# A chunked linear-attention kernel with two gated layers: the queries' table of powers moves to PSUM and scales seven chunks of keys backwards on DVE

## The chip, the cores and the metric

The kernel runs on one core of a Trainium2 chip. The metric is the device time of one execution in microseconds (us). The core's engines each run their own instructions in order: TensorE (PE, with PEld loading weights), VectorE (DVE), ScalarE (ACT), GpSimd (POOL), and SyncE (SP), which issues all transfers here.

## The reference, cut to what matters

```python
# attention with per-channel decay: B=4, 8 heads, S=768, 48 channels per head
for t in range(S):
    cur = einsum('bhd,bhe->bhde', u * k_t, v_t)
    y[:, :, t] = einsum('bhd,bhde->bhe', r_t, state + cur)
    state = w * state + einsum('bhd,bhe->bhde', k_t, v_t)
x = y laid out as (B, S, 384)
# first layer: u, v = halves of relu(x @ w_in); v is normalised over its channels
v_s = einsum('ts,bsd->btd', w_spatial, v_n) + b_spatial
x = (u * v_s) @ w_out
# second layer: h = relu(x @ w_in2); convolution of 3 taps along the sequence
out = (h * sigmoid(conv(h))) @ w_out2
```

Everything is fp32. Each large product of the layers is computed from split operands (a rounded part and its remainder), as three matmuls into one accumulation.

## The kernel before, in words

The attention goes through 24 chunks of 128 positions, six for each of four batches. Chunk n has two tiles: `ld` (queries and keys with channels on partitions, 112 x 2 x 4 x 128) and `nat` (queries, keys and values with positions on partitions). Three of each are in flight; the load of chunk n+3 is issued after chunk n's last matmul.

The decay inside a chunk is put into the operands. `tables` (L508) fills TT in SBUF: TT[:, 0] holds w^(t-64) for the queries, TT[:, 1] w^(63-s) for the keys. `scaled` (L569) multiplies the queries of chunk n by TT[:, 0] on DVE (L574); `scaled_k` (L581) multiplies the keys by TT[:, 1] on POOL (L583), but for chunk 0, where DVE does both at once (L578). Then:

- `products` (L211, line L216) writes keys times queries into two PSUM banks, `pa0` and `pa1`, one for each head of a pair;
- `masked` (L618, line L621) copies what lies on the allowed side of the diagonal from `pa` to `aT` on DVE; `aT` was filled by ACT (L254) with the diagonal that belongs to `u`;
- `outer` (L235, line L239) writes keys times values of the chunk into the bank `pu`; `state` (L677) adds it to `zc` on DVE (L683, L685), ACT writes it to `zbd` (L245), and POOL applies the decay (L692);
- `from_state` (L219, line L222) and `from_chunk` (L225, line L231) build the output in the bank `py`; ACT and DVE split it into `ys` and `xT` (L658 to L662), and a part of it goes through DRAM: a write to `yd` (L667), then two reads into `xT` (L672).

The first layer has `s1` (L720, half of w_in, one chunk at a time, then a normalisation on DVE and ACT), `s2` (L764, the other half), `s3` (L784, the spatial product) and `s4` (L810); the second layer has `s5` (L887) and `s6` (L933). The weights come as 64-bit words in disguise: DVE converts a block of them in four instructions (L427 to L430, tile `wy`), and ACT and POOL split it (L362, L364).

The program is written out by a planner (class `Order`): every piece of work is a generator that names the engine and a cost, waits for keys (`need`) and free slots (`take`), and the planner emits instructions in the order in which its model starts them. So a change in what waits for what changes the order of all five engines. Until a planned time of 62 us the planner fills gaps on PE with matmuls whose result is not used (`keep_warm`, L558, line L565). All eight PSUM banks are in use: three for the layers (`ps_m`), one for the weight conversion, `pa0`, `pa1`, `py` and `pu`.

Of the kernel before, what the change touches and what calls it, by code (L numbers as in the profile page):

```python
# [26 lines left out]
class Order:  # L27
# [58 lines left out]
    def spawn(self, g, rank=1, at=None):  # L86
        self._go(g, rank, self.t if at is None else at, None)
# [61 lines left out]
class Net:  # L149
# [26 lines left out]
            fill=0.0, base=0, channel_multiplier=-1)  # L176
        nc.gpsimd.memset(self.zbd, 0.0)

    def att_psum(self, ps):
        C, NP = self.C, self.NP  # L180
        self.pa = [ps.tile([C, NP, C], F32, name=f"pa{i}") for i in range(2)]
        self.py = ps.tile([self.R, NP, C], F32, name="py")
        self.pu = ps.tile([self.R, NP, self.D], F32, name="pu")
        self.nc.vector.memset(self.py, 0.0)
        self.nc.vector.memset(self.pu, 0.0)

    def powers(self, asc, dsc, n):

# [159 lines left out]
    def run(self, xd=None):  # L348
# [130 lines left out]
        if xd is None:  # L479
            ac = right("ac", 1)  # L480
            ld_p, nat_p = right("ld", 3), right("nat", 3)
            ew_p, at_p, ys_p = right("ew", 2), right("at", 2), right("ys", 2)
            TT = ac.tile([R, 2, NP, C], F32, name="TT")
            W128 = ac.tile([R, NP, 1], F32, name="W128")
            mask = ac.tile([C, C], U32, name="mask")
            maskb = mask.rearrange("c (o t) -> c o t", o=1).to_broadcast([C, NP, C])
            yd = dram.tile([n_chunks, R, 2 * C], F32, name="yd")
            W128b = W128.to_broadcast([R, NP, D])
# [19 lines left out]
        def tables():  # L508

            asc = x2_p.tile([R, NP, HALF + 1], F32, tag="x2", name="asc")  # L510
            dsc = x2_p.tile([R, NP, HALF + 1], F32, tag="x2", name="dsc")
            wt = ew_p.tile([R, 4, NP], F32, tag="wt", name="wt")
            dw = t_p.tile([R, NP, R], F32, tag="t", name="dw")
            wr, w2, m, wk = (wt[:, i] for i in range(4))
            m = m.bitcast(U32)
            iv = ew_p.tile([R, NP, 1], F32, tag="iv", name="iv")
            nc.sync.dma_start(out=wr, in_=self.wq)
            nc.gpsimd.memset(dsc[:, :, HALF:HALF + 1], 1.0)
            self.att_consts(ac)
            nc.sync.dma_start(out=self.uB, in_=self.u.broadcast_to([C, DM]))  # L520
            nc.vector.memset(asc[:, :, 0:1], 1.0)

            nc.vector.memset(wk, 1.0)
            self.att_psum(att.enter_context(tc.tile_pool(name="ps_a", bufs=1, space=PSUM)))

            for _ in range(4):
                nc.tensor.matmul(
                    out=self.pa[1][0:R, :, 0:R], lhsT=self.zbd[:, 0], rhs=self.zbd, start=True, stop=True)
            nc.vector.tensor_tensor(w2, wr, wr, ALU.mult)
            nc.vector.tensor_scalar(m, w2, W2_MIN, None, ALU.is_ge)  # L530
            nc.vector.scalar_tensor_tensor(m, w2, W2_MAX, m, ALU.is_le, ALU.mult)
# [7 lines left out]
            nc.vector.tensor_tensor(TT[:, 0, :, 0:HALF], asc[:, :, 0:HALF], ivb, ALU.mult)
            nc.vector.tensor_tensor(TT[:, 1, :, HALF:C], dsc[:, :, 1:HALF + 1], ivb, ALU.mult)  # L540
            nc.scalar.activation(out=TT[:, 0, :, HALF:C], in_=asc[:, :, 0:HALF], func=ACTF.Copy)
            nc.scalar.activation(out=TT[:, 1, :, 0:HALF], in_=dsc[:, :, 1:HALF + 1], func=ACTF.Copy)

            for p in range(NP):
                nc.scalar.activation(
                    out=dw[:, p], in_=self.ident[0:R, 0:R], func=ACTF.Copy, scale=W128[:, p])
            self.transpose_table(TT[:, 1], dw)

        def masks():
            yield gps(3 * C, 3)  # L550
# [17 lines left out]

        def scaled(n):  # L569
            yield need(("ldd", n))  # L570
            if n:
                spawn(scaled_k(n), rank(n))
                yield dve(NP * C)
                nc.vector.tensor_tensor(ld[n][:, 0], ld[n][:, 0], TT[:, 0], ALU.mult)  # L574
                done(("lq", n))
            else:
                yield dve(2 * NP * C)
                nc.vector.tensor_tensor(ld[n], ld[n], TT, ALU.mult)  # L578
                done(("lq", n), ("lk", n))

        def scaled_k(n):  # L581
            yield gps(NP * C)
            nc.gpsimd.tensor_tensor(ld[n][:, 1], ld[n][:, 1], TT[:, 1], ALU.mult)  # L583
            done(("lk", n))

        def bonus(n):
# [21 lines left out]

        def att_a(n):
            yield need(("lq", n), ("lk", n))  # L610
            yield need(("A", n - 1, 0), ("A", n - 1, 1))
            yield od.pairs(1.0)
            self.products(ld[n][:, 0], ld[n][:, 1])
            for x in range(2):
                spawn(masked(n, x), rank(n))
            yield FORK

        def masked(n, x):  # L618
# [5 lines left out]
        def att_v(n):  # L624
            b, c = divmod(n, NCH)
            on = c < NCH - 1
            yield need(("lq", n), ("kn", n), ("z", n - 1))
            if on:
                yield od.pairs(0.45)
                self.outer(nat[n][:, 1], nat[n][:, 2])  # L630
                spawn(state(n), rank(n))
            yield need(("y", n - 1))
            if c:
                yield od.pairs(1.0)
                self.from_state(ld[n][:, 0])
            done(("mix", n))
            yield need(("A", n, 0), ("A", n, 1))
            if c % HC == 0:
                yield take(x_f)
            yield take(ys_f)  # L640
# [36 lines left out]
        def state(n):  # L677
            first = n % NCH == 0
            if not first:
                yield need(("zw", n - 1))  # L680
            yield dve(NP * D)
            if first:
                nc.vector.tensor_copy(out=self.zc, in_=self.pu)  # L683
            else:
                nc.vector.tensor_tensor(self.zc, self.zc, self.pu, ALU.add)  # L685
            yield need(("mix", n))
            yield act(2 * NP * D, 2)
            self.set_state()
            done(("z", n))
            if n % NCH < NCH - 2:  # L690
                yield gps(NP * D)
                nc.gpsimd.tensor_tensor(self.zc, self.zc, W128b, ALU.mult)  # L692
                done(("zw", n))
# [263 lines left out]
                        break  # L957
                spawn(g, rank(i))

        done(("A", -1, 0), ("A", -1, 1), ("z", -1), ("y", -1))  # L960
# [40 lines left out]
        if xd is None:  # L1001
# [121 lines left out]
```

## Time and profile before

| what | value |
|---|---|
| three runs | 602.73, 599.0, 602.54 us (median 602.54) |
| profiled execution | 605.17 us, of which the span of instructions 603.1 us |
| PE busy | 577.6 us (96%), 3980 matmuls |
| DVE / ACT / POOL busy | 382.3 (63%) / 356.5 (59%) / 291.2 us (48%) |
| mean granted TensorE clock | 0.976 |

The times of the runs are of separate executions; the profiled one is 2.6 us longer than their median. In the tables of the trace, "idle before" is the time in which an engine stood still just before an instruction, with what released it. The granted clock of TensorE is a share of full speed: 1.00 is 2.4 GHz, 0.50 is 1.2 GHz, and values between are means over a stretch.

### The profile page before, as it was taken

How to read it: one execution, taken by the hardware profiler on the slowest of the kernel's cores; microseconds unless marked ns; L12 is line 12 of the kernel's file. 1: busy time of each engine (PE TensorE's matmuls, PEld its weight loads, DVE VectorE, ACT ScalarE, POOL GpSimd, SP SyncE). 2: the span in 40 equal slices, each digit the busy share in tenths (PEclk: the TensorE clock that was granted, in tenths of full speed). 3: DMA queues.
4: the chain of work that ended last, by engine and by line, in shares of the span. 5: the costliest groups of instructions: out<-in, count | busy, mean ns of one | idle time of the engine just before them, and what ended most of it. 6: DMA issues, size and time to landing. Idle time of an engine off the chain costs nothing.

```text
span 603.1 us, 11155 instructions
## 1 busy us (share of the span) xinstructions
PE 577.6 (96%) x3980; PEld 546.3 (91%) x3980; DVE 382.3 (63%) x864; ACT 356.5 (59%) x877; POOL 291.2 (48%) x315
## 2 busy tenths in 40 slices
PE   6999969999999999999999999999999999999992
PEld 3999858999888999888999999999999999999991
DVE  4889878867679847778665533675546455564701
ACT  3558766736586456486354524487667666675810
POOL 5688877855858329468414240254223243232410
PEclk8999969999999999999999999999999999999997
DMA  8676545546565456285346714340221303120010
GB/s 219 209 218 210 153 158 163 172 140 212 156 194 195 114 165 217 57 265 160 120 166 238 261 59 139 150 158 27 93 84 49 106 13 106 57 76 27 15 39 33
DMA packets 49316, 81.29 MB, mean 135 GB/s; under 512 B 5601, under 2 KB 40930, under 8 KB 48866
## 3 DMA queue, kind: packets, MB, share of 16 engines
q1 hardware_dynamic: 49250, 80.48, 42.3%
q8 instruction: 33, 0.54, 0.4%
q14 instruction: 33, 0.27, 0.1%
HBM read 57.27 MB, written 23.20 MB: 133 GB/s over the span
## 4 chain that ended last, share of the span: by engine, by line
PE 88%; POOL 3%; DMA 3%; DVE 2%; issue 1%; ACT 1%; SPq 0%; ACTq 0%; DVEq 0%; POOLq 0%
PE s L887 17%; PE s L933 17%; PE s L784 15%; PE s L720 9%; PE s L810 8%; PE s L764 7%; PE pa L216 4%; PE warm L565 4%; PE py L231 4%; PE py L222 2%; DMA ld<-in_rkT_dram 1%; PE pu L239 1%; DMA nat<-in_rkv_dram 1%; POOL nat L591 1%; POOL ld L583 1%
## 5 line engine op out<-in xcount | busy, mean ns | idle before, releaser
L364 POOL TENSOR_TENSOR g<-g,g 128x384 fp32r<-128x384 f32 x64 | 64.6, 1014 | 122.6 <-ACT g L362 122.6
L887 PE MATMUL s<-xl,wi 128*128 128x386 f32 x576 | 108.1, 340 | 0.0
L933 PE MATMUL s<-wo,g 128*128 128x384 f32 x576 | 107.0, 339 | 0.0
L784 PE MATMUL s<-wsp,vn 128*128 128x384 f32 x576 | 104.3, 337 | 0.4 <-POOL vn L364 0.4
L887 PEld LDWEIGHTS s<-xl,wi 128*128 128x128 f32 x576 | 102.5, 189 | 0.0
L933 PEld LDWEIGHTS s<-wo,g 128*128 128x128 f32 x576 | 102.1, 188 | 0.0
L784 PEld LDWEIGHTS s<-wsp,vn 128*128 128x128 f32 x576 | 99.7, 188 | 2.4 <-POOL vn L364 0.8
L900 DVE SCALAR_TENSOR_TENSOR c<-h,cw,c 128x384 f32<-128x384 f32 x64 | 39.7, 621 | 57.6 <-ACT c L898 57.6
L254 ACT ACTIVATE aT<-ident,dg 128x128 f32<-128x128 f32 x192 | 60.1, 392 | 9.3 <-DVE dg L249 9.0
L364 POOL TENSOR_TENSOR gat<-u,gat 128x384 fp32r<-128x384 f32 x32 | 32.6, 1027 | 53.7 <-ACT gat L362 49.4
L720 PE MATMUL s<-wi,xT 128*128 128x512 f32 x216 | 57.2, 415 | 0.0
L764 PE MATMUL s<-xT,wi 128*128 128x384 f32 x288 | 54.7, 338 | 0.0
L810 PE MATMUL s<-gat,wo 128*128 128x384 f32 x288 | 53.3, 337 | 0.0
L764 PEld LDWEIGHTS s<-xT,wi 128*128 128x128 f32 x288 | 50.0, 188 | 1.0 <-ACT zbd L245 0.2
L810 PEld LDWEIGHTS s<-gat,wo 128*128 128x128 f32 x288 | 50.0, 188 | 0.6 <-ACT zbd L245 0.2
L720 PEld LDWEIGHTS s<-wi,xT 128*128 128x128 f32 x216 | 41.6, 198 | 9.5 <-issue 0.2
L903 ACT ACTIVATE c<-c 128x384 f32<-128x384 f32 x64 | 29.7, 465 | 31.5 <-DVE c L901 31.5
L907 DVE TENSOR_TENSOR g<-h,c 128x384 f32<-128x384 f32 x64 | 35.2, 551 | 19.9 <-ACT c L903 18.8
L895 ACT ACTIVATE h<-s 128x386 f32<-128x386 f32 x64 | 31.3, 489 | 17.1 <-PE s L887 15.9
L901 DVE SCALAR_TENSOR_TENSOR c<-h,cw,c 128x384 f32<-128x384 f32 x64 | 39.9, 623 | 2.3
L591 POOL TENSOR_TENSOR nat<-nat 128x384 f32<-128x384 f32 x24 | 24.9, 1039 | 31.6 <-DMA nat<-in_rkv_dram 23.3
L364 POOL TENSOR_TENSOR stg<-stg 128x192 fp32r<-128x192 f32 (+1 forms) x34 | 19.8, 587 | 41.2 <-ACT stg L362 35.7
(103 smaller groups left out, 932.1 us busy)
## 6 DMA issues: line engine op xcount, KB each, us to landing
nat<-in_rkv_dram SPq DMA_DIRECT2D x24, 576.0 KB, 4.2
ld<-in_rkT_dram SPq DMA_DIRECT2D x24, 448.0 KB, 5.4
xl<-x2d SPq DMA_DIRECT2D x8, 1155.0 KB, 6.1
x2d<-x SPq DMA_DIRECT2D x24, 384.0 KB, 3.0
stg<-in_w_out_dram SPq DMA_DIRECT2D x24, 192.0 KB, 2.8
out_dram<-o SPq DMA_DIRECT2D x24, 192.0 KB, 1.9
stg<-in_w_in_dram SPq DMA_DIRECT2D x12, 256.0 KB, 3.9
wo2d<-stg SPq DMA_DIRECT2D x16, 192.0 KB, 1.9
```

The costliest lines, as they stand in the source:

```text
L254: self.nc.scalar.activation(out=a[:, x, h // 2], in_=self.ident, func=ACTF.Copy, scale=d[:, h:h + 1])
L364: nc.gpsimd.tensor_tensor(dst[1], src, dst[0].bitcast(F32), ALU.subtract)
L720: nc.tensor.matmul(out=ps, lhsT=xt[:, k, l], rhs=wi[:, k, r, UF:DFF], start=(k == 0 and (l, r) == PARTS[0]), stop=(k == KD - 1 and (l, r) ...
L764: nc.tensor.matmul(out=ps, lhsT=wi[:, k, l, f * 128:(f + 1) * 128], rhs=xT[b, h][:, k, :, r], start=(k == 0 and (l, r) == PARTS[0]), stop= ...
L784: nc.tensor.matmul(out=ps, lhsT=vn[:, s, l, f * 128:(f + 1) * 128], rhs=wsp[:, s, r, h * HT:(h + 1) * HT], start=(s == 0 and (l, r) == PAR ...
L810: nc.tensor.matmul(out=ps, lhsT=wo[:, k, l, m * 128:(m + 1) * 128], rhs=gat[b, h, k][:, r], start=(k == 0 and (l, r) == PARTS[0]), stop=(k ...
L887: nc.tensor.matmul(out=ps, lhsT=late["wi2"][:, k, l, f * 128:(f + 1) * 128], rhs=xl[j][:, k, r], start=(k == 0 and (l, r) == PARTS[0]), st ...
L895: nc.scalar.activation(out=h, in_=ps, func=ACTF.Relu)
L900: nc.vector.scalar_tensor_tensor(c, h[:, 0:HT], cw[:, f, 0:1], c, ALU.mult, ALU.add)
L901: nc.vector.scalar_tensor_tensor(c, h[:, 2:HT + 2], cw[:, f, 2:3], c, ALU.mult, ALU.add)
L907: nc.vector.tensor_tensor(g, h[:, 1:HT + 1], c, ALU.mult)
L933: nc.tensor.matmul(out=ps, lhsT=g2[j][:, k, l, t * 128:(t + 1) * 128], rhs=late["wo2"][:, k, r], start=(k == 0 and (l, r) == PARTS[0]), st ...
```

## The change: what it does

1. The queries' table moves to a PSUM bank, `TQ`; the keys' table stays in SBUF as `TK`.
2. Read backwards, TQ gives w^(63-s), the keys' powers. For chunks 0 to 6 DVE scales queries and keys in two instructions, both with TQ; from chunk 7 on POOL scales the keys with TK, as before.
3. TQ takes the bank of `pu`. The outer product now goes into the first 192 columns of `pa0`. So `outer` of chunk n has to wait until `masked` has copied `pa0` of chunk n (key `("A", n, 0)`), and `products` of chunk n+1 until `zc` has taken the outer product (new key `("zc", n)`).
4. `outer` becomes a piece of its own (`att_o`), in one chain with `att_a` (the products).

```diff
-    def att_psum(self, ps):
+    def att_psum(self, ps, own=True):
         self.pa = [ps.tile([C, NP, C], F32, name=f"pa{i}") for i in range(2)]
         self.py = ps.tile([self.R, NP, C], F32, name="py")
-        self.pu = ps.tile([self.R, NP, self.D], F32, name="pu")
...
+        else:
+            pu = self.pa[0].rearrange("c p t -> c (p t)")[0:self.R, 0:NP * self.D]
+            self.pu = pu.rearrange("r (p d) -> r p d", p=NP)
...
-            TT = ac.tile([R, 2, NP, C], F32, name="TT")
+            TK = ac.tile([R, NP, C], F32, name="TK")
...
+            TQ = TT["q"] = ps_a.tile([R, NP, C], F32, name="TQ")
...
         def scaled(n):
             yield need(("ldd", n))
-            if n:
+            late_k = n >= 7
+            if late_k:
                 spawn(scaled_k(n), rank(n))
+            yield dve(NP * C)
+            nc.vector.tensor_tensor(ld[n][:, 0], ld[n][:, 0], TT["q"], ALU.mult)
+            done(("lq", n))
+            if not late_k:
                 yield dve(NP * C)
-                nc.vector.tensor_tensor(ld[n][:, 0], ld[n][:, 0], TT[:, 0], ALU.mult)
-                done(("lq", n))
-            else:
-                yield dve(2 * NP * C)
-                nc.vector.tensor_tensor(ld[n], ld[n], TT, ALU.mult)
-                done(("lq", n), ("lk", n))
+                nc.vector.tensor_tensor(ld[n][:, 1], ld[n][:, 1], TT["q"][:, :, ::-1], ALU.mult)
+                done(("lk", n))
...
         def att_a(n):
             yield need(("lq", n), ("lk", n))
-            yield need(("A", n - 1, 0), ("A", n - 1, 1))
+            yield need(("A", n - 1, 0), ("A", n - 1, 1), ("zc", n - 1))
...
+        def att_o(n):
+            if n % NCH == NCH - 1:
+                done(("zc", n), ("o", n))
+                return
+            yield need(("kn", n), ("A", n, 0))
+            yield od.pairs(0.45)
+            self.outer(nat[n][:, 1], nat[n][:, 2])
+            done(("o", n))
+            spawn(state(n), rank(n))
+            yield FORK
...
         def att_v(n):
             yield need(("lq", n), ("kn", n), ("z", n - 1))
-            if on:
-                yield od.pairs(0.45)
-                self.outer(nat[n][:, 1], nat[n][:, 2])
-                spawn(state(n), rank(n))
...
-            yield need(("A", n, 0), ("A", n, 1))
+            yield need(("A", n, 0), ("A", n, 1), ("o", n))
...
+            done(("zc", n))
...
-            for g in (att_a, att_v):
-                spawn(od.chain([(g(n), rank(n)) for n in range(n_chunks)]), 0)
+            for gs in ((att_a, att_o), (att_v,)):
+                spawn(od.chain([(g(n), rank(n)) for n in range(n_chunks) for g in gs]), 0)
```

The planner's new order differs on every engine. Three places matter. In the rows, the matmuls of `products` alternate between `pa_159` (pa0) and `pa_160` (pa1), four of each for a chunk; a line of "..." leaves out the repeats.

PE at the end of the first batch, before: from the last matmuls of chunk 5 (`py`) to the second of the two `s1` products (tiles s_1066 and s_1171) that end batch 0.

```order
L231 MATMUL py<-aT,nat 48x128 x8
L216 MATMUL pa_159<-ld 128x128
...
L239 MATMUL pu<-nat 48x48 x8
L720 MATMUL s_1066<-wi,xT 128x512 x9
L231 MATMUL py<-aT,nat 48x128 x8
L216 MATMUL pa_159<-ld 128x128
...
L239 MATMUL pu<-nat 48x48 x8
L720 MATMUL s_1171<-wi,xT 128x512 x9
```

The same place in the changed kernel (the two `s1` products are s_1069 and s_1155):

```order
L227 MATMUL py<-ld,zbd 112x128 x4
L574 MATMUL warm<-ident 128x128 x2
L236 MATMUL py<-aT,nat 48x128 x8
L738 MATMUL s_1069<-wi,xT 128x512 x9
L221 MATMUL pa_159<-ld 128x128
...
L738 MATMUL s_1155<-wi,xT 128x512 x9
L244 MATMUL pa_159<-nat 48x48 x8
```

The second `s1`, which works on chunk 5's own output, now comes after one `s1` and one set of products; before, two sets of products, one `py`, two outer products and one `s1` stood between. Over the whole order the matmuls of L565 rise from 98 to 112.

DVE in the same stretch, before: the two masked copies of chunk 5 follow each other, and between those of chunk 6 stand the statistics of `s1` and a scaling of queries.

```order
L621 COPY_PREDICATED aT<-mask,pa_159 128x512
L621 COPY_PREDICATED aT<-mask,pa_160 128x512
...
L621 COPY_PREDICATED aT<-mask,pa_159 128x512
L733 BN_STATS s_1105<-v 128x6
L734 BN_AGGR mv<-s_1105 128x2
L736 TENSOR_SCALAR rs<-mv 128x1
L574 TENSOR_TENSOR ld<-ld,TT 112x512
L621 COPY_PREDICATED aT<-mask,pa_160 128x512
```

DVE in the changed kernel: the masked copies of chunk 5, then the scalings of chunk 6's queries (L584) and keys (L588).

```order
L642 COPY_PREDICATED aT<-mask,pa_159 128x512
L432 TENSOR_SCALAR wy<-stg 128x192
...
L435 SCALAR_TENSOR_TENSOR stg<-stg,wy 128x192
L642 COPY_PREDICATED aT<-mask,pa_160 128x512
...
L584 TENSOR_TENSOR ld<-ld,TQ 112x512
L254 TENSOR_REDUCE dg<-nat 128x8
L678 TENSOR_TENSOR ys<-py,ys 112x128
L679 TENSOR_TENSOR xT<-py,xT 112x3x128
L588 TENSOR_TENSOR ld<-ld,TQ 112x512
```

A block of four weight conversions now stands between the copies of chunk 5, and the statistics no longer stand between those of chunk 6.

PE in the third batch, before, around chunk 13's output (first row) and the state product of chunk 14 (L222):

```order
L231 MATMUL py<-aT,nat 48x128 x8
L764 MATMUL s_2232<-xT,wi 128x384 x9
L239 MATMUL pu<-nat 48x48 x8
L222 MATMUL py<-ld,zbd 112x128 x4
L231 MATMUL py<-aT,nat 48x128 x8
```

And in the changed kernel:

```order
L236 MATMUL py<-aT,nat 48x128 x8
L244 MATMUL pa_159<-nat 48x48 x8
L227 MATMUL py<-ld,zbd 112x128 x4
L221 MATMUL pa_159<-ld 128x128
```

The `s2` product that stood between chunk 13's output and the outer product of chunk 14 has moved away.

## Rows read from the trace of the kernel before

**Rows 1.** The page, part 1: busy us (share of span) x instructions.

```profile
PE 577.6 (96%) x3980; PEld 546.3 (91%) x3980; DVE 382.3 (63%) x864; ACT 356.5 (59%) x877; POOL 291.2 (48%) x315
```

**Rows 2.** Waits of PE: who waited for whom, total us, times, longest.

```profile
PE py L231 <- DVE rs L740: 5.0, 1, 5.0
...
PE pa L216 <- POOL vn L364: 1.5, 1, 1.5
PE pa L216 <- POOL gat L364: 1.2, 1, 1.2
```

**Rows 3.** Stretches: us, busy time by engine, granted clock (PEclk), DMA.

```profile
12.40:14.60 2.20, 2.09 (x17) 1.90 (x17) 0.50 (x2) 1.74 (x6) 2.14 (x4) 0.50 1.03 298
18.00:20.00 2.00, 2.00 (x19) 1.98 (x18) 1.86 (x5) 0.85 (x3) 1.62 (x3) 0.98 0.33 118
73.00:74.40 1.40, 0.00 (x0) 0.02 (x1) 1.40 (x2) 1.29 (x4) 1.40 (x2) 1.00 0.28 83
76.00:78.00 2.00, 2.00 (x9) 1.61 (x6) 2.00 (x5) 1.24 (x5) 2.00 (x3) 0.52 1.01 324
78.00:80.00 2.00, 2.00 (x8) 1.28 (x6) 0.97 (x2) 0.20 (x1) 2.00 (x3) 0.62 1.00 322
84.00:86.00 2.00, 0.72 (x8) 0.71 (x10) 1.89 (x7) 0.57 (x2) 1.44 (x2) 0.50 0.00 0
92.00:94.00 2.00, 2.00 (x9) 1.62 (x8) 1.52 (x5) 0.19 (x1) 1.78 (x2) 0.71 0.44 123
243.00:245.00 2.00, 0.92 (x6) 0.60 (x4) 2.00 (x2) 0.64 (x3) 2.00 (x3) 1.00 0.01 5
```

**Rows 4.** Chain of waits in order of time: start us, us, what.

```profile
22.77 2.88 PE warm L565 x24
...
40.95 1.09 PE pa L216 x16
...
55.20 2.08 PE s L720 x9
...
60.46 1.06 PE py L222 x8
```

**Rows 5.** Groups by line and shape: busy us, mean ns, idle before.

```profile
L565 PE MATMUL warm<-ident 128*128 128x128 f32 x196 | 25.4, 287 | 0.0
L574 DVE TENSOR_TENSOR ld<-ld,TT 112x512 f32<-112x512 f32 x23 | 32.9, 1431 | 2.5 <-DMA ld<-in_rkT_dram 2.5
L793 DVE TENSOR_TENSOR u<-s,u 128x384 f32<-128x384 f32 x32 | 17.8, 557 | 1.4
L428 DVE SCALAR_TENSOR_TENSOR wy<-stg,wy 128x192 uint32<-128x192 uint32 x39 | 14.1, 362 | 1.3
L583 POOL TENSOR_TENSOR ld<-ld,TT 112x512 f32<-112x512 f32 x23 | 32.2, 1401 | 0.0
```

**Rows 6.** DVE and POOL in order of time: start us, us, instruction.

```profile
62.45 1.38 DVE L621 COPY_PREDICATED aT<-mask,pa 128x512 f32<-128x512 uint32 x2
63.37 0.75 POOL L364 TENSOR_TENSOR wi<-stg,wi 128x256 fp32r<-128x256 f32 x1
63.95 0.70 DVE L574 TENSOR_TENSOR ld<-ld,TT 112x512 f32<-112x512 f32 x1
81.65 2.94 DVE L574 TENSOR_TENSOR ld<-ld,TT 112x512 f32<-112x512 f32 x1
```

**Rows 7.** Chunk 0's output on its way back, in order of time; transfers: median us to landing.

```profile
20.10 1.08 PE L231 MATMUL py<-aT,nat 128*48 128x128 f32 x16
22.15 0.55 DVE L662 TENSOR_TENSOR xT<-py,xT 112x384 fp32r<-112x384 f32 x1
22.26 0.33 SPq L667 DMA_DIRECT2D yd<-ys  x1
25.83 0.83 SPq L672 DMA_DIRECT2D xT<-yd  x2
xT<-yd SPq DMA_DIRECT2D x48, 48.0 KB, 2.5
```

More of the change, by code (lines that the diff above doesn't have):

```diff
@@ L182, in att_psum @@
         self.py = ps.tile([self.R, NP, C], F32, name="py")
-        self.pu = ps.tile([self.R, NP, self.D], F32, name="pu")
         self.nc.vector.memset(self.py, 0.0)
-        self.nc.vector.memset(self.pu, 0.0)
+        if own:
+            self.pu = ps.tile([self.R, NP, self.D], F32, name="pu")
+            self.nc.vector.memset(self.pu, 0.0)
+        else:
+            pu = self.pa[0].rearrange("c p t -> c (p t)")[0:self.R, 0:NP * self.D]
+            self.pu = pu.rearrange("r (p d) -> r p d", p=NP)
     def powers(self, asc, dsc, n):
@@ L482, in run @@
             ew_p, at_p, ys_p = right("ew", 2), right("at", 2), right("ys", 2)
-            TT = ac.tile([R, 2, NP, C], F32, name="TT")
+            TK = ac.tile([R, NP, C], F32, name="TK")
+            TT = {}
             W128 = ac.tile([R, NP, 1], F32, name="W128")
@@ L523, in tables @@
             nc.vector.memset(wk, 1.0)
-            self.att_psum(att.enter_context(tc.tile_pool(name="ps_a", bufs=1, space=PSUM)))
+            ps_a = att.enter_context(tc.tile_pool(name="ps_a", bufs=1, space=PSUM))
+            self.att_psum(ps_a, False)
+            TQ = TT["q"] = ps_a.tile([R, NP, C], F32, name="TQ")
             for _ in range(4):
@@ L538, in tables @@
             nc.vector.reciprocal(out=iv, in_=asc[:, :, HALF:HALF + 1])
[L539 to L542, printed above, removed]
+            nc.vector.tensor_tensor(TQ[:, :, 0:HALF], asc[:, :, 0:HALF], ivb, ALU.mult)
+            nc.vector.tensor_tensor(TK[:, :, HALF:C], dsc[:, :, 1:HALF + 1], ivb, ALU.mult)
+            nc.scalar.activation(out=TQ[:, :, HALF:C], in_=asc[:, :, 0:HALF], func=ACTF.Copy)
+            nc.scalar.activation(out=TK[:, :, 0:HALF], in_=dsc[:, :, 1:HALF + 1], func=ACTF.Copy)
             for p in range(NP):
@@ L546, in tables @@
                     out=dw[:, p], in_=self.ident[0:R, 0:R], func=ACTF.Copy, scale=W128[:, p])
-            self.transpose_table(TT[:, 1], dw)
+            self.transpose_table(TK, dw)
         def masks():
@@ L570, in scaled @@
             yield need(("ldd", n))
-            if n:
+            late_k = n >= 7
+            if late_k:
                 spawn(scaled_k(n), rank(n))
+            yield dve(NP * C)
+            nc.vector.tensor_tensor(ld[n][:, 0], ld[n][:, 0], TT["q"], ALU.mult)
+            done(("lq", n))
+            if not late_k:
                 yield dve(NP * C)
-                nc.vector.tensor_tensor(ld[n][:, 0], ld[n][:, 0], TT[:, 0], ALU.mult)
-                done(("lq", n))
-            else:
-                yield dve(2 * NP * C)
-                nc.vector.tensor_tensor(ld[n], ld[n], TT, ALU.mult)
-                done(("lq", n), ("lk", n))
+                nc.vector.tensor_tensor(ld[n][:, 1], ld[n][:, 1], TT["q"][:, :, ::-1], ALU.mult)
+                done(("lk", n))
         def scaled_k(n):
             yield gps(NP * C)
-            nc.gpsimd.tensor_tensor(ld[n][:, 1], ld[n][:, 1], TT[:, 1], ALU.mult)
+            nc.gpsimd.tensor_tensor(ld[n][:, 1], ld[n][:, 1], TK, ALU.mult)
             done(("lk", n))
@@ L958, in in_turn @@
                 spawn(g, rank(i))
-        done(("A", -1, 0), ("A", -1, 1), ("z", -1), ("y", -1))
+        done(("A", -1, 0), ("A", -1, 1), ("z", -1), ("y", -1), ("zc", -1))
         by_gat = gat_p, "g", gat_f, 2 * HT
```

## The prediction, made before the changed kernel had run

> **What bounds the kernel now.** I read the busy times first: PE works 577.6 of 603.1 us, and no other engine comes near [rows 1]. Then the waits of PE: in the whole program it stands still for 5.0, 1.5 and 1.2 us once each, and hardly otherwise after the start [rows 2]. So the time is the sum of PE's own work plus these stops, plus what a low clock costs. Third, the stretches around the stops: after the stop of 1.5 us (the empty row at 73.00) the granted clock is 0.52 and 0.62 from 76 to 80, which makes 1.92 + 1.52 = 3.4 us at half speed, 1.7 us lost. The stop of 5.0 us ends at 85.3; from there the clock is at 1.2 GHz until about 93.2 (0.71 in 92 to 94 is 1.16 us of low clock), 7.9 us, so 4.0 us lost. The stop of 1.2 us, in the row at 243.00, brought no fall of the clock [rows 3]. Lost in all: 1.5 + 1.7 + 5.0 + 4.0 + 1.2 = **13.4 us**. That is everything this change can win on PE; the rest of the matmuls stay as they are.
>
> Fourth, the other engines at these stops. The query scaling on DVE (both factors in SBUF) takes 1431 ns on average, though one alone takes 0.70 us; one of 2.94 us stands right in front of the masked copy for which PE waited 5.0 us [rows 5, 6]. Instructions with one factor in PSUM, as L793, average 557 ns for 384 columns with 1.4 us of idle in 32 [rows 5]. That is what the change attacks: DVE with two SBUF operands waits for POOL.
>
> **The change part by part.**
>
> *Scaling.* 23 query scalings fall from 1431 ns to about 700 (the 0.70 us of one that was not held up; L793 scaled by 512/384 would give 743 [rows 5, 6]). DVE gains 23 x 0.73 = 17 us, and pays 7 x 0.70 = 4.9 us for keys, of which chunk 0's were there before. POOL loses six scalings of 1.40 us. None of it lies on PE's path except through the stops above. A backward read of PSUM stands in no row; I bound it by 0.70 and by the 1431 ns of the old query scaling, and take 0.70, since nothing in L793 says that a PSUM read is slow. The Trainium skill speaks against the move (Perfetto Trace Analysis, Optimizing Scalar/DVE Operations): it gives DVE about 60 ns of access overhead on SBUF and 125 on PSUM. By that the 31 scalings would cost 2.0 us more on DVE, and the sum would be the same; L793 shows no more than 743 - 700 = 43 ns of it.
>
> *Idle matmuls.* The new order holds 112 instead of 98 matmuls of L565, each two rows of the trace (196 now). 24 rows take 2.88 us, so 28 more take **3.4 us** [rows 4, 5]. They stand where PE did not wait before, so nothing hides them: PE runs them whether or not anybody is late.
>
> *Chunk 5's copies.* On DVE four weight conversions (4 x 0.36 = 1.45 us) now stand between the two masked copies (0.69 each): 2.8 us from the end of the products to the second copy [rows 5, 6]. On PE only a state product (1.06) and two idle matmuls (0.48) lie between [rows 4]. PE stops for **1.3 us**. Before, the copies of chunk 5 followed each other; chunk 6 had the 5.0 us stop in just this way, and that one goes.
>
> *The way of chunk 5's output.* The second `s1` of the new order needs chunk 5's output, which goes through DRAM. For chunk 0 the matmuls end at 21.18, the write is issued at 22.26, the second read at about 26.2, and a read lands 2.5 us later: 28.7, that is 7.5 us [rows 7]. PE now has 2.08 + 1.09 = 3.2 us of work in between [rows 4]; before, the stop of 5.0 us and low-clock work lay there. PE stops for **4.3 us**. Lower bound 3.9, if the landing counts from the first of the two reads (25.83); upper bound 6.4, if the subtraction also queues behind four conversions and a scaling (2.1 us) [rows 5, 6]. The Trainium skill (DMA: Bandwidth & Descriptors, Anatomy of one DMA) gives a transfer about 2.0 us plus bytes over 436 GB/s. By that the 115 KB write would land after 2.3 us, and the sum would be 1.3 us lower; the read was issued 3.57 us after the write, so I keep the trace [rows 7].
>
> *The clock.* After that stop the clock is low again: 4.0 us were lost after the stop of 5.0, about 2.8 us at the program's start (0.50 from the products at 12.5 to about 18 [rows 3]). I take **3.4 us**; nothing at the low end. A fall after the 1.3 us stop would be hidden, since what it slows lies inside the 7.5 us of the output's way.
>
> *Chunk 14.* Its state product needs chunk 13's output to be split: 22.70 - 21.18 = 1.5 us on ACT and DVE [rows 7]. The `s2` that covered this has moved; only the outer product remains, shorter than a state product's 1.06 us [rows 4]. PE stops for 0.5 to 1.5, I take **1.0 us**.
>
> *The shared bank.* Between the masked copy and the outer product, and between `zc` and the next products, the new order leaves PE other work nearly everywhere. What is queued behind the waiting `zc` on DVE is weight conversion, which PE needs later. I cost this at nothing; the cover is the layers' matmuls in between.
>
> *The 1.2 us stop.* POOL still scales those later keys; I leave **1.2 us** in.
>
> Sum: 3.4 + 1.3 + 4.3 + 3.4 + 1.0 + 1.2 = 14.6 us of idle matmuls, stops and low clock in place of 13.4: **+1.2 us**. The profiled execution of 605.17 us would become 606.4; the median of the runs, 602.54, becomes 603.7. With all low ends (3.9, no fall of the clock, 0.5, no late stop) it is 3.4 + 1.3 + 3.9 + 0.5 - 13.4 = -4.3, so 598.2; with the high ends (6.4, 4.0, 1.5, and 1.7 for a clock that falls after chunk 5's stop and is not hidden) 19.5 - 13.4 = +6.1, so 608.6.
>
> **Rivals.**
>
> *A late weight block (slower).* In the new order five key scalings, 5 x 0.70 = 3.5 us, stand on DVE ahead of the twelfth block of w_in. POOL ends that block at 64.1 in the trace before [rows 6]; the first `s2` that needs it comes soon after. For it: DVE is the engine that these blocks go through. Against it: as many query scalings get 0.73 us shorter, and 3.4 us of idle matmuls bring PE there later. If both covers fail, PE stops 3.5 us there and the clock falls once more (4.0): 603.7 + 7.5 = 611.2. It decides from a stop of about 2.4 us on: with 2.8 for the clock that is 5.2, past 1% above the time before. Chance 0.20.
>
> *The clock holds.* After a stop of 1.2 us it did not fall [rows 3]; if it also holds after 4.3 us, the sum loses 3.4: 600.3. Against it: it fell after 1.5 and after 5.0. Chance 0.13.
>
> *All stops at 73 to 93 go (faster).* With a DVE that never waits for POOL, PE might run through: 3.4 - (1.5 + 1.7 + 5.0 + 4.0) = -8.8, so 593.7. It speaks for it that a held-up scaling stood before the longest stop; against it that 7.5 us of way do not fit in 3.2 us of work. Chance 0.07.
>
> *The scaling is held up all the same.* If the PSUM table does not free DVE of POOL, each key on DVE costs 1.4 us: 5 x 0.73 = 3.7 us later at the weight blocks, of which the idle matmuls cover 3.4: some 604 to 607. L793 speaks against it. Chance 0.05.
>
> **How the numbers follow.** My forecast (same within 1%) has 0.55, at 603.7. The range takes in the clock that holds and most of the late block: 598.5 to 610.0. About 1%, 6 us, is what a measurement of this kernel can tell from no change. Faster by more than that: the rival at 593.7 with a little for what I did not see, 0.08. Slower: the late block, 0.20. Within 1%: 0.72.
>
> **What would show it.** Right: a mean of about 0.7 us for both scalings on DVE, none above 1 us; 224 rows of idle matmuls; a stop before chunk 5's `py`, one of about 4 us before the second `s1` after it, with the clock at 0.5 behind it; a stop of 1 us before chunk 14's state product. Wrong: no stop at that `s1` (the output's way is shorter than I read it), or stops at `s2` or at outer products before 72 us (then DVE is late), or scalings above 1 us (then PSUM does not free DVE).

## The result: slower by 1.4%

| kernel | median of its runs, us | ratio to the kernel before, 95% interval | profiled execution (span), us |
|---|---|---|---|
| before | 601.6 (599.0 to 602.7) | 1 | 605.17 (603.1) |
| before, a second profiled execution | | | 601.85 (599.2) |
| changed | 609.4 (608.1 to 609.9) | 1.0136 [1.0094, 1.0178] | 609.88 (608.1) |

The time lies in the range (598.5 to 610.0), at its upper end. The case that I held likeliest, no change within 1% at 603.7, did not come; the time is 5.7 us above it. Where the time is spent is read from one profiled execution of each kernel, and executions differ by some us, as the two of the kernel before show.

### The profile page after: what moved, and what is told of

Its sections match the earlier page's. It is cut to its first block, busy times and chain, and to the rows that moved or that the text cites. A ratio compares the mean times of both kernels' runs of the same rounds, so it can differ in the third digit from the quotient of the medians.

```text
span 608.1 us, 11219 instructions
## 1 busy us (share of the span) xinstructions
PE 582.4 (96%) x4008; PEld 547.6 (90%) x4008; DVE 370.1 (61%) x870; ACT 356.5 (59%) x877; POOL 274.8 (45%) x309
## 4 chain that ended last, share of the span: by engine, by line
PE 91%; DMA 3%; DVE 2%; ACT 2%; issue 1%; SPq 0%; POOL 0%; DVEq 0%; ACTq 0%
PE s L905 17%; PE s L951 17%; PE s L802 17%; PE s L738 9%; PE s L828 8%; PE s L782 8%; PE warm L574 5%; PE pa L221 4%; PE py L236 3%; PE py L227 3%; DMA ld<-in_rkT_dram 2%; PE pa L244 1%; DMA xT<-yd 0%; ACT v L764 0%; ACT aT L259 0%
## 5 line engine op out<-in xcount | busy, mean ns | idle before, releaser
L802 PE MATMUL s<-wsp,vn 128*128 128x384 f32 x576 | 106.1, 341 | 1.6 <-ACT vn L367 0.9
L802 PEld LDWEIGHTS s<-wsp,vn 128*128 128x128 f32 x576 | 101.1, 190 | 3.8 <-ACT vn L367 1.2
L782 PE MATMUL s<-xT,wi 128*128 128x384 f32 x288 | 56.1, 341 | 0.0
L738 PEld LDWEIGHTS s<-wi,xT 128*128 128x128 f32 x216 | 40.2, 192 | 13.5 <-issue 4.7
L369 POOL TENSOR_TENSOR vn<-v,vn 128x512 fp32r<-128x512 f32 x24 | 30.7, 1288 | 30.7 <-ACT vn L367 30.5
L642 DVE COPY_PREDICATED aT<-mask,pa 128x512 f32<-128x512 uint32 x48 | 34.7, 742 | 10.8 <-PE pa L221 5.8
```

The lines of the kernel that those rows point to most:

```text
L369: nc.gpsimd.tensor_tensor(dst[1], src, dst[0].bitcast(F32), ALU.subtract)
L642: nc.vector.copy_predicated(aT[n][:, x], maskb, self.pa[x])
L738: nc.tensor.matmul(out=ps, lhsT=xt[:, k, l], rhs=wi[:, k, r, UF:DFF], start=(k == 0 and (l, r) == PARTS[0]), stop=(k == KD - 1 and (l, r) ...
L782: nc.tensor.matmul(out=ps, lhsT=wi[:, k, l, f * 128:(f + 1) * 128], rhs=xT[b, h][:, k, :, r], start=(k == 0 and (l, r) == PARTS[0]), stop= ...
L802: nc.tensor.matmul(out=ps, lhsT=vn[:, s, l, f * 128:(f + 1) * 128], rhs=wsp[:, s, r, h * HT:(h + 1) * HT], start=(s == 0 and (l, r) == PAR ...
```

## The profile after

The busy times, in answer to [rows 1]: DVE has 12.2 us less and POOL 16.4 less, as meant; PE has 4.8 us more, nearly all of it idle matmuls.

```profile
PE 582.4 (96%) x4008; PEld 547.6 (90%) x4008; DVE 370.1 (61%) x870; ACT 356.5 (59%) x877; POOL 274.8 (45%) x309
```

Groups of instructions by line and shape (busy us, mean ns, idle before), in answer to [rows 5]. Both scalings on DVE take 0.68 us, forwards and backwards. The 28 more rows of idle matmuls add 4.9 us of busy time, in which matmuls overlap; at 0.12 us from one row to the next they hold PE for 3.4. POOL's own key scaling has become shorter too, 1287 for 1401 ns.

```profile
L574 PE MATMUL warm<-ident 128*128 128x128 f32 x224 | 30.3, 292 | 0.0
...
L593 POOL TENSOR_TENSOR ld<-ld,TK 112x512 f32<-112x512 f32 x17 | 21.9, 1287 | 1.3 <-DMA ld<-in_rkT_dram 1.3
...
L584 DVE TENSOR_TENSOR ld<-ld,TQ 112x512 f32<-112x512 f32 x24 | 16.3, 679 | 10.7 <-DMA ld<-in_rkT_dram 10.7
...
L588 DVE TENSOR_TENSOR ld<-ld,TQ 112x512 f32<-112x512 f32 x7 | 4.7, 677 | 0.0
```

PE's waits (who for whom, total us, times, longest), in answer to [rows 2]. Three stops stand where the prediction put them: 4.1 us at the `s1` that needs chunk 5's output, 1.1 before chunk 5's `py`, 1.4 before chunk 14's state product. The stop of 1.2 us at the later keys is gone. The last two rows were not foreseen: `s3` of the last batch waits for its normalised operand `vn`.

```profile
PE s L738 <- DMA xT<-yd: 4.1, 1, 4.1
...
PE py L227 <- DVE xT L679: 1.4, 1, 1.4
PE py L236 <- DVE aT L642: 1.1, 1, 1.1
PE s L802 <- ACT vn L367: 0.9, 1, 0.9
PE s L802 <- POOL vn L369: 0.7, 1, 0.7
```

Stretches (us, busy by engine, granted clock, DMA), in answer to [rows 3]. The clock falls to 0.50 (1.2 GHz) twice: behind the stop at `s1`, and behind the stop at `s3` (the low clock at the program's start left aside). The shares below 1.00 make 0.58 + 1.00 + 0.12 = 1.7 us lost for the first and 0.48 + 1.00 + 0.24 = 1.7 for the second.

```profile
86.00:88.00 2.00, 1.47 (x4) 1.26 (x5) 1.93 (x5) 1.97 (x6) 2.00 (x3) 0.71 0.01 4
88.00:90.00 2.00, 2.00 (x6) 1.33 (x5) 1.74 (x5) 0.89 (x4) 1.72 (x3) 0.50 0.00 0
90.00:92.00 2.00, 2.00 (x25) 1.61 (x24) 0.88 (x2) 0.85 (x2) 0.60 (x1) 0.94 0.64 197
...
352.00:354.00 2.00, 1.31 (x5) 1.32 (x6) 0.80 (x2) 0.00 (x0) 0.63 (x1) 0.76 1.04 383
354.00:356.00 2.00, 2.00 (x8) 2.00 (x7) 0.33 (x1) 0.52 (x1) 1.00 (x1) 0.50 0.10 34
356.00:358.00 2.00, 2.00 (x11) 2.00 (x11) 0.15 (x1) 0.00 (x0) 0.00 (x0) 0.88 0.00 0
```

The unforeseen stop in order of time (start us, us, instruction). The last `s1` ends at 346.1. Its way through ACT and DVE, then to `vn`, ends on ACT at 351.3 and on POOL at 352.6. PE has one `s2` and 15 matmuls of `s3` to do meanwhile, and stands at the sixteenth.

```profile
341.89 2.27 PE L828 MATMUL s<-gat,wo 128*128 128x384 f32 x12
344.00 2.24 PE L738 MATMUL s<-wi,xT 128*128 128x512 f32 x9
346.08 1.75 PE L782 MATMUL s<-xT,wi 128*128 128x384 f32 x9
347.66 2.77 PE L802 MATMUL s<-wsp,vn 128*128 128x384 f32 x15
...
350.65 0.63 ACT L367 ACTIVATE vn<-v 128x512 fp32r<-128x512 f32 x1
351.33 0.62 PE L802 MATMUL s<-wsp,vn 128*128 128x384 f32 x2 [0.91 <-ACT vn L367]
351.36 1.27 POOL L369 TENSOR_TENSOR vn<-v,vn 128x512 fp32r<-128x512 f32 x1 [1.69 <-ACT vn L367]
352.69 1.67 PE L802 MATMUL s<-wsp,vn 128*128 128x384 f32 x5 [0.73 <-POOL vn L369]
```

In the kernel before, the last two `s1` follow each other (the 18 matmuls ahead of these rows), and behind them come an `s2` and an `s4`:

```profile
342.26 1.75 PE L764 MATMUL s<-xT,wi 128*128 128x384 f32 x9
343.84 2.24 PE L810 MATMUL s<-gat,wo 128*128 128x384 f32 x12
345.92 3.11 PE L784 MATMUL s<-wsp,vn 128*128 128x384 f32 x17
```

From the start of that `s2` to the start of `s3` that is 3.7 us of cover, where now 1.6 are left (346.08 to 347.66), since the `s4` slipped in between the two `s1`.

**Where the time went.** For each unbroken run of matmuls of one kind, the table takes the time up to the start of the next run, less what such a run takes at full clock without a stop (products 1.09 us, `s1` 2.06, `s2` 1.56, `s3` 3.12, an idle row 0.12, and so on). What is left, summed by stretch, is stops, low clock and the small cost of changing from one kind to another.

| us lost on PE | 12 to 20 | 20 to 70 | 70 to 95 | 95 to 340 | 340 to 400 | after | PE ends at |
|---|---|---|---|---|---|---|---|
| before, first execution | 2.6 | -0.5 | 12.3 | 5.3 | 0.8 | 0.3 | 591.2 |
| before, second execution | 3.0 | -0.5 | 8.0 | 6.3 | 0.8 | 0.3 | 587.8 |
| changed | 3.2 | -0.2 | 8.7 | 6.8 | 3.9 | 0.3 | 595.9 |

Against the second execution PE ends 8.2 us later (before rounding): 3.4 from 28 idle rows, 3.1 at `s3`, 0.7 at 70 to 95, 0.6 at 95 to 340, the rest before 70. The medians of the runs differ by 7.8. Against the first execution it ends 4.7 later.

## Experiments

All times below are medians. The ratios, with their 95% intervals, are to the kernel before, which ran beside each experiment (its medians lie between 601.2 and 601.8 us). Differences from the changed kernel compare medians of runs at different times. Where they are 3.3 us or less (runs 1 and 4), the intervals of the two ratios overlap, and the trace has to say what changed.

**1. Fewer idle matmuls.** The order is the changed kernel's.

```diff
+            i = 0
...
-                for j in range(2):
+                i += 1
+                for j in range(0 if i % 7 == 1 and i > 1 else 2):
```

> The changed kernel with the same order on every engine, but 7 of the 56 idle pieces (14 matmuls, 28 rows of the trace) are not issued; 98 matmuls are left, as in the kernel before. Theory (the idle matmuls stand on PE's path and hide nothing): 28 rows x 0.12 us = 3.4 us less, 606.0 us against 609.4 of the changed kernel, 1.007 of the kernel before; the stops before chunk 5's py (1.1) and before the s1 that needs chunk 5's output (4.1) stay. Rival (DVE, the weights or the scalings are late there anyway): PE only arrives earlier and stops longer between 20 and 72 us; the time stays within 1 us of 609.4.

Measured: 606.15 us, 1.0084 [1.0053, 1.0116], 3.3 us below the changed kernel. PE ends at 592.3, 3.7 earlier. The stop of about 4 us at the second `s1` stays at 4.2, so it only moved earlier with everything else, and the loss at 20 to 70 us goes from -0.2 to 0.7: the idle matmuls stand on PE's path and these 14 covered next to nothing.

**2. The table in SBUF.** The same order on every engine.

```diff
-            TQ = TT["q"] = ps_a.tile([R, NP, C], F32, name="TQ")
+            TQ = TT["q"] = ac.tile([R, NP, C], F32, name="TQ")
```

> The changed kernel with the same order on every engine; only the queries' table TQ lies in SBUF and no longer in PSUM. Theory (DVE with two SBUF operands is held up by POOL, PSUM frees it): the mean of the 24 query scalings goes from 679 ns back to 1.2 to 1.4 us, that of the 7 key scalings on DVE from 677 ns to about the same, single ones to 2 us and more; DVE is busy for some 15 to 20 us more, weight conversions come later, and the time rises by 2 to 8 us to 611 to 617. Rival (the place of the table is of no account): 0.68 to 0.72 us each, the time within 1 us of 609.4.

Measured: 622.82 us, 1.0343 [1.03, 1.0386], 13 us above the changed kernel, more than expected. Its groups (same columns as above):

```profile
L584 DVE TENSOR_TENSOR ld<-ld,TQ 112x512 f32<-112x512 f32 x24 | 37.2, 1551 | 8.9 <-DMA ld<-in_rkT_dram 8.9
...
L593 POOL TENSOR_TENSOR ld<-ld,TK 112x512 f32<-112x512 f32 x17 | 24.1, 1418 | 0.0
...
L588 DVE TENSOR_TENSOR ld<-ld,TQ 112x512 f32<-112x512 f32 x7 | 6.1, 869 | 0.0
```

The queries are back at 1551 ns and POOL at 1418: the PSUM table is what keeps the two engines out of each other's way. The keys on DVE, 869 ns, suffer less than I expected. PE pays for it at places where the changed kernel does not stop at all. The profiled execution, at 617.51 us one of the two shortest of six, loses 10 us more than the changed kernel at 95 to 340 us; its longest new wait is this one, for a masked copy that stands on DVE behind a query scaling of 5.67 us, and the clock falls behind it (0.72 and 0.50 from 124 to 128 us):

```profile
PE pa L244 <- DVE aT L642: 4.1, 1, 4.1
```

```profile
118.02 5.67 DVE L584 TENSOR_TENSOR ld<-ld,TQ 112x512 f32<-112x512 f32 x1
123.61 1.33 DVE L642 COPY_PREDICATED aT<-mask,pa 128x512 f32<-128x512 uint32 x2
```

**3. The second `s1` later.** The planner is told that chunk 5's output comes later.

```diff
+            if n == 5:
+                yield "X", 0.0, 4.0
             done(("x", b, c))
```

> The changed kernel; the planner is told that chunk 5's output arrives 4.0 us later, so that the s1 that needs it stands behind outer 5, chunk 6's output and the products of chunk 7 (0.5 + 1.0 + 1.1 us). Theory (that stop is way minus work): the stop of 4.1 us falls to about 1.5, and the clock loss of 1.7 us behind it goes if the stop is short enough: 2.6 to 4.3 us less, 605.1 to 606.8. Rival (DVE is the limit there, the stop only moves): PE then stops before chunk 6's py or the products of chunk 7 for the masked copies and zc, 2 us or more in all; the time 608 to 610.

Measured: 610.7 us, 1.0157 [1.0128, 1.0187]: no gain, as the rival had it, but at `outer`. PE's waits:

```profile
PE pa L244 <- DVE aT L642: 5.4, 1, 5.4
...
PE s L740 <- DMA xT<-yd: 0.3, 1, 0.3
```

The `s1` no longer waits for the transfer. In its place the outer product of chunk 6 stands 5.4 us for a masked copy, which is at the end of DVE's queue:

```profile
80.38 0.69 DVE L753 BATCH_NORM_STATS2 s<-v 128x6 f32<-128x512 f32 x1
...
81.39 0.35 DVE L432 TENSOR_SCALAR wy<-stg 128x192 uint32<-128x192 uint32 x1
...
83.79 0.35 DVE L432 TENSOR_SCALAR wy<-stg 128x192 uint32<-128x192 uint32 x1
...
85.24 0.73 DVE L642 COPY_PREDICATED aT<-mask,pa 128x512 f32<-128x512 uint32 x1
```

So two waits lie side by side at 80 to 87 us, the output's way through DRAM and DVE's queue of normalisation and weight conversions. The one hides the other, and taking one away gains nothing. That `outer` waits for a masked copy at all is the shared bank's doing: with a bank of its own it needs none.

**4. The last pair of `s1` together.** One `s4` waits for the last `s1`, which gives the order of the kernel before at this place.

```diff
+            done(("s1", b, c))
...
+            if (b, h, m) == (2, 1, 2):
+                yield need(("s1", B - 1, NCH - 1))
```

> The changed kernel; one s4 (batch 2, second half, third block) waits for the last s1. The last two s1 then stand together with an s2 and an s4 behind them, as in the kernel before; all rows of PE before that place are the same. Theory (the s3 stop at 348 us comes from this order: 1.6 us of work behind the last s1 where 3.8 stood): the stop of 1.6 us and the fall of the clock at 353 us (1.7 us lost) go, 3.3 us less, 606.1. Rival (an accident of the profiled execution): the time stays within 1 us of 609.4 and other executions never had that stop.

Measured: 607.44 us, 1.0094 [1.0063, 1.0126], 2.0 below the changed kernel where 3.3 were expected, a difference that the two intervals alone do not settle. The trace does: the stop at `s3` has shrunk to 0.4 and the clock stays at 1.00 there; the loss at 340 to 400 us is 0.8 again, as before the change. In this run's profiled execution the stop at `s1` was 5.8 us instead of 4.1, so that PE ends only 1.5 earlier. The stop is no accident: it is there, with 0.9 and 0.7 us, in the runs 1, 2, 5, 6, 8 and 12 as well, and in two parts of 0.7 and 0.6 us in the runs 3 and 7.

**5. Half of the idle matmuls.**

```diff
+            i = 0
...
-                for j in range(2):
+                i += 1
+                for j in range(0 if i > 6 and i % 2 else 2):
```

> The changed kernel with the same order on every engine, but every second idle piece from the seventh on is not issued: 62 idle matmuls are left of 112, 100 rows of the trace fewer. Theory (the idle matmuls are PE time and nothing else as long as DVE keeps up): up to 100 x 0.12 = 12 us less, 597.4; DVE stands idle for 10 us in all between 20 and 75 us, so that some of it may come back as stops; 597 to 602. Rival (they cover what the other engines need): PE stops in their place between 20 and 72 us, the clock falls behind the stops, and less than 4 us is left: 605 or more.

Measured: 603.95 us, 1.0049 [1.0017, 1.0081]: 5.5 us gained of 12, between theory and rival. New stops of 2.7, 2.6 and 0.9 us stand before 70 us, where PE now comes too early; the loss at 20 to 70 us goes from -0.2 to 7.5. So a few of them hide nothing (run 1), and of a large cut more than half comes back as stops.

**6. The shared bank and the chain alone**, on the kernel before: table and keys as before. Of the edit the two new waits are shown; `outer` also moves into `pa0` and into the chain, as in the change.

```diff
...
-            yield need(("A", n - 1, 0), ("A", n - 1, 1))
+            yield need(("A", n - 1, 0), ("A", n - 1, 1), ("zc", n - 1))
...
-            yield need(("A", n, 0), ("A", n, 1))
+            yield need(("A", n, 0), ("A", n, 1), ("o", n))
...
```

> The kernel before with the shared bank and the new chain alone: outer writes into pa0 and waits for the masked copy, the products wait for zc; the table stays in SBUF with both halves, POOL scales the keys from chunk 1 on, 96 idle matmuls. Theory (sharing costs nothing, as I took it; what counts is the new order): stops before outer and before the products for zc stay under 1 us in all after 20 us, the time within 4 us of the kernel before (601.8), by whatever stops its order brings around 75 to 90 us. Rival (the sharing is what made the change slower): stops at outer (for the masked copy) and at the products (for zc) of 3 us or more, 606 to 612.

Measured: 608.37 us, 1.0112 [1.0067, 1.0158]: the time of the rival, but not its cause. No stop stands at `outer` for a masked copy, none at the products for `zc`. The longest, after the program's first products, is this one (order of time):

```profile
62.90 4.87 DVE L578 TENSOR_TENSOR ld<-ld,TT 112x512 f32<-112x512 f32 x1
63.70 1.08 PE L235 MATMUL py<-aT,nat 128*48 128x128 f32 x16
...
67.82 2.08 PE L220 MATMUL pa<-ld 48*128 48x128 f32 x16 [3.05 <-DVE ld L578]
```

One query scaling in SBUF takes 4.87 us and PE stands 3.05 for it; the clock is at 0.50 behind it, from 68 to 74 us. It also has the stop at `s3`. No wait for the bank itself shows here; the order that comes with the sharing costs, together with the table in SBUF.

**7. Keys on POOL from chunk 1 on.**

```diff
-            late_k = n >= 7
+            late_k = n >= 1
```

> The changed kernel, but POOL scales the keys from chunk 1 on, as before; the queries' table stays in PSUM and the bank stays shared; 108 idle matmuls by the planner. Theory (the PSUM table is what gains, keys on DVE are no help): the query scalings stay at 0.68 us, DVE has six scalings of 0.68 us less before 85 us, and the time is below 609.4 by the 4 idle matmuls (1 us) and a shorter stop around 80 us: 604 to 608. Rival (POOL's 1.4 us key scalings hold up the products): stops before products for POOL's ld, 1 us or more each, 609 to 614.

Measured: 602.22 us, 1.0029 [0.9996, 1.0061], 7.2 below the changed kernel, better than the theory's range. No stop for POOL's keys. PE ends at 587.2: of 8.7 us, 4.3 come at 70 to 95 (stops of 0.9, 1.4 and 1.0, the clock stays up), 1.5 at `s3`, 1.4 before 20 us, 1.0 from eight idle rows. This mixes two things, another place of the keys and another order; run 12 parts them.

**8. The masked copies first**, together with the later `s1` of run 3.

```diff
-                spawn(masked(n, x), rank(n))
+                spawn(masked(n, x), 0.005)
```

> The changed kernel with chunk 5's output planned 4.0 us later, as in the run where outer stood still for 5.4 us, and with the masked copies ahead of every weight block in the planner's ranks. Theory A (PE simply has no work as long as chunk 5's output is under way): outer no longer waits for a masked copy behind weight conversions, but the s1 behind the products of chunk 7 stops instead, way 7.5 minus work 3.7 = 3.8 us; the time stays at 608 to 611. Theory B (DVE's queue is the cause, chunk 6's masked copy waits behind 4.9 us of normalisation and weight conversions): both stops fall under 1.5 us and 4 us or more are gained, 605 or less.

Measured: 608.78 us, 1.0118 [1.007, 1.0166], the time of theory A but the wait of neither. PE's waits:

```profile
PE pa L221 <- DVE ld L588: 6.8, 2, 3.8
...
PE pa L244 <- DVE aT L642: 1.5, 1, 1.5
```

Of the first row 3.0 us belong to the program's first products, as in the other kernels, and 3.8 to the products of chunk 6, which wait for their key scaling. With the copies first, the scalings are late: it is DVE's whole queue there, not one instruction in it.

**9. The kernel before once more.**

> The kernel before, unchanged, for a second profiled execution. Theory (the execution profiled first, 605.17 us, was an unlucky one: 3 us above the median of its runs, so that subtracting 2.6 us carried that over to the forecast): 599 to 603 us, with one of the stops at 72 to 93 us or the fall of the clock behind it shorter by 2 to 4 us. Rival (the profiled execution is slower by nature): about 605 again, with the same stops of 1.5, 5.0 and 1.2 us.

Measured: 601.85 us, a single run, the theory. The same stops are there, two of the three shorter, with one of 0.7 us besides, and with the clock low for 3.4 us in this stretch instead of 13.7:

```profile
PE py L231 <- DVE rs L740: 3.8, 1, 3.8
...
PE pa L216 <- POOL gat L364: 1.3, 1, 1.3
PE pa L216 <- POOL vn L364: 0.9, 1, 0.9
PE py L231 <- DVE aT L621: 0.7, 1, 0.7
```

```profile
76.00:78.00 2.00, 1.64 (x8) 0.99 (x6) 2.00 (x5) 1.54 (x5) 2.00 (x3) 1.00 1.03 329
82.00:84.00 2.00, 1.47 (x16) 1.10 (x17) 1.85 (x7) 1.81 (x7) 2.00 (x3) 0.79 0.16 52
84.00:86.00 2.00, 2.00 (x20) 1.78 (x22) 0.71 (x2) 1.97 (x6) 1.18 (x2) 0.50 0.57 131
```

At 76 to 78 us the clock is at 1.00 where it was at 0.52 [rows 3]. 4.3 us of the loss at 70 to 95 us belonged to the first execution alone.

**10 and 11. A version that beats both.** The kernel of run 7, with every third (10) or every second (11) idle piece from the seventh on left out, and one `s4` held back so that two `s4` stand behind the last `s1`. The edit of run 10 against the changed kernel; run 11 has `i % 2`:

```diff
+            i = 0
...
-                for j in range(2):
+                i += 1
+                for j in range(0 if i > 6 and i % 3 == 0 else 2):
...
-            late_k = n >= 7
+            late_k = n >= 1
...
+            done(("s1", b, c))
...
+            if (b, h, m) == (2, 1, 1):
+                yield need(("s1", B - 1, NCH - 1))
```

> Table in PSUM and shared bank as in the changed kernel, keys on POOL from chunk 1 on (602.2 us as measured), every third idle piece from the seventh on not issued (76 matmuls left of 108, 64 rows, 7.7 us), and one s4 held back so that two s4 stand behind the last s1. Theory: the s3 stop and its clock fall go (2 us), of the 7.7 us at least the share that the run with half of them gained (5.5 of 12) stays: 593 to 597, faster than the kernel before. Rival (PE only waits longer for DVE and POOL): 600 or more.

> As the run before it, with every second idle piece left out (58 or so left). Theory: by the run with 62 idle matmuls, stops come back for more than half of it; against the run with 76 it gains 0 to 2 us: 592 to 597. Rival (each idle matmul left out is a gain): 590 to 591.

Measured: 596.5 us, 0.9921 [0.9892, 0.995], and 596.42 us, 0.9918 [0.9885, 0.9952]. Both are faster than the kernel before by 0.8%, and within the bands of their theories, near the upper ends. The stop at `s3` is gone (0.04 us lost at 340 to 400). Of the 76 idle matmuls that run 10 still has, leaving out 16 more gains nothing: the loss at 20 to 70 us rises from 3.0 to 6.1.

**12. The keys on POOL in the changed kernel's order.**

```diff
-                nc.vector.tensor_tensor(ld[n][:, 1], ld[n][:, 1], TT["q"][:, :, ::-1], ALU.mult)
+                if n:
+                    nc.gpsimd.tensor_tensor(ld[n][:, 1], ld[n][:, 1], TK, ALU.mult)
+                else:
+                    nc.vector.tensor_tensor(ld[n][:, 1], ld[n][:, 1], TT["q"][:, :, ::-1], ALU.mult)
```

> The changed kernel with its order kept to the instruction, 112 idle matmuls and the s3 stop included; only the key scalings of chunks 1 to 6 are issued on POOL (table TK) at the place where DVE had them. Theory (the keys on DVE lengthen DVE's queue in front of what PE waits for at 76 to 87 us): DVE has two scalings of 0.68 us less between 78 and 82 us and four before, so that the stops at 76 to 93 us shrink by 1.4 to 2 us and the fall of the clock with them or not: 606 to 608. Rival 1 (it was the planner's order that gained in the run with the keys on POOL, not DVE's time): 609.4 within 1 us. Rival 2 (POOL, busy without a break at 75 to 80 us, brings the keys later than DVE did): stops before products for POOL's ld of 1.4 us or more, 610 to 613.

Measured: 609.3 us, 1.0136 [1.0089, 1.0184], the same as the changed kernel: rival 1. PE's waits:

```profile
PE s L741 <- ACT v L767: 3.3, 1, 3.3
...
PE s L805 <- ACT vn L367: 0.9, 1, 0.9
PE pa L221 <- POOL ld L589: 0.8, 1, 0.8
PE s L805 <- POOL vn L369: 0.7, 1, 0.7
```

The stop at `s1` is 0.8 shorter, and the products wait 0.8 for POOL's key. (The first row names ACT; by the landing times the reads of chunk 5's output land 0.13 us before this `s1` starts, as in the changed kernel.) Whether DVE or POOL scales the keys is of no account here. Of the 7 us between this kernel and that of run 7, 1.0 are four idle matmuls fewer; the rest is the order, which the planner changes when it is told that the keys cost POOL time instead of DVE time.

## Why the prediction was right or wrong, point by point

- **Scaling: right.** 679 ns forwards and 677 backwards for the predicted 0.70 each; run 2 shows that PSUM does it, and no price of reading PSUM shows against the 0.70 us in SBUF. **What it is worth to PE: too low.** The prediction let the table count only at the stops of the old order. In the new order the time without it is 13 us longer (run 2), with a stop at an outer product that neither the kernel before nor the changed one has.
- **Idle matmuls: right.** 3.4 predicted, 3.3 in run 1.
- **Chunk 5's copies: right**, 1.1 for 1.3. **Chunk 14: near**, 1.4 for 1.0.
- **The way of chunk 5's output: right in size**, 4.1 for 4.3, but only half of the mechanism. Runs 3 and 8 show DVE's queue right beside it, so that shortening the way alone would hardly have won anything. The estimate of 2.3 us for the write, which the prediction sets beside its own, rests on a section of the Trainium skill (DMA: Bandwidth & Descriptors, Anatomy of one DMA) whose fit is for transfers issued by GpSimd; here SyncE issues them, and the write landed after 3.1 to 5.2 us.
- **The clock: mis-sized for this execution.** 3.4 predicted, 1.7 measured behind that stop. I took it from the one execution in which the clock stayed low for 7.9 us behind the stop. Worked out in the same way, the low clock behind this stop cost 3.0 us in run 1, 2.6 in run 4 and 1.7 in the runs 5 and 12, so that one execution does not give its size.
- **The 1.2 us stop: wrong**, it went. The new order has other work there.
- **The shared bank at nothing: right for this kernel's waits, not for its time.** The changed kernel and run 6 have no stop for the bank, but the runs 2, 3 and 8 have: 4.1, 5.4 and 1.5 us at `outer`, as soon as DVE is late or the order another. And a new order came with it. By medians, each step with its own order: the bank and the chain alone make the kernel before some 7 us slower (run 6), the table in PSUM then makes it 6 us faster (run 7), and the seven chunks of keys on DVE 7 us slower again, the change's +7.8.
- **Where it failed, first: "the rest of the matmuls stay as they are".** I read the new order at the places where PE had stopped before. At the end of the attention's work an `s4` had moved between the last two `s1`, and the `s3` behind them lost its cover: 1.6 us of stop and 1.7 of clock in the profiled execution, 3.1 us by the table, 2.0 us by the medians of run 4. My sum of stops and idle matmuls, 14.6, was 11.7 at the places that it names (3.4 + 1.1 + 4.1 + 1.7 + 1.4) and 15.0 with these 3.3.
- **Where it failed, second: the 13.4 us "lost before".** They were one execution's. The second one (run 9) lost 4.3 less at 70 to 95 us. Taking 2.6 us off at the end, to come to the median, gave back only part of that: the changed kernel's profiled execution stands 0.5 above its median. In numbers: against the first execution PE ends 4.7 us later where I had 1.2, and 3.1 of those 3.5 are the `s3` stop and its clock. The other 2.2 of the 5.7 us come from the 2.6 that I took off, where only 0.5 was to be taken off. The two executions of the kernel before lie 3.4 apart (591.2 and 587.8).
- **The range: held by luck.** With all high ends my sum came to 608.6; the range reached up to 610.0 for the late weight block, which did not come. The time got there by the `s3` stop, which I had not foreseen.
- **The rivals.** The late weight block did not come: no stop at an `s2` or `outer` before 72 us. The clock did not hold behind the 4.1 us stop. The scaling was not held up.

Open: the 2.0 us of run 4 and the 3.1 of the table probably differ by what the clock and the stop at `s1` did in single executions. Why a switch of order by the planner's costs is worth 4.3 us at 70 to 95 us in run 7 was seen in its stops, not taken apart further.

## What to carry to other kernels

- Where a planner writes the order, an edit's price is the new order's: ask at every producer with a long way (here the last `s1` to `vn`, and chunk 5's output through DRAM) how much work now stands behind it, up to the end of the program, not only where there were stops before. Run 12 against run 7 shows 6 us of order beside 1 us of idle matmuls.
- Losses that are read from one profiled execution carry that execution's luck; where it lies above the median, look which stop and which low clock could be the surplus before any of it is booked as something to win.
- Here DVE and POOL hold each other up when both multiply in SBUF at once (1551 against 679 ns on DVE, 1418 against 1287 on POOL); the operand in PSUM was worth 13 us in the new order, and yet the change as a whole lost, by what the bank had done before and by the order.

## What the runs showed of the hardware that I had not expected

- The same write in the same order lands after very different times. From the issue of chunk 5's write to the issue of its read, which waits for it, it is 3.17 us in the changed kernel, 3.65 in run 12, 3.79 in run 1, 4.77 in run 5 and 5.24 in run 4; the stop at `s1` is 4.1, 3.3, 4.2, 5.1 and 5.8. By the landing times in these five traces the write lands 0.25 to 0.53 us after the load of `nat` that SP had issued 1.0 to 1.6 us before it, and the reads land 0.2 to 0.5 us after the load of `ld` that it issued between. So what differs is probably the loads ahead in the queue; no run issues the write before them, so that is not shown.
- The same stop brings a fall of the clock or not. Behind the `s3` stop of 0.9 + 0.7 us the clock was at 0.50 in the changed kernel and at 0.51 in run 12; in the runs 1, 2, 5, 6 and 8 it stayed at 1.00. Run 1:

```profile
350.00:352.00 2.00, 1.45 (x8) 1.45 (x9) 0.93 (x2) 0.00 (x0) 0.50 (x1) 1.00 1.02 376
352.00:354.00 2.00, 2.00 (x14) 2.00 (x13) 0.19 (x1) 0.53 (x1) 1.01 (x1) 1.00 0.14 49
354.00:356.00 2.00, 2.00 (x13) 2.00 (x12) 1.12 (x2) 0.53 (x1) 0.05 (x1) 1.00 0.00 0
```
